# Attention and MLP on one core: the first 128 tokens of four batches ahead of everything, as the first MLP chunk

## The chip, the core, the metric

One NeuronCore of a Trainium2 chip runs the whole kernel. The metric is device time in microseconds (us), the median of several executions. A profile shows one execution; its span is 1.7 to 2.1 us shorter than that execution's time. Ratios are computed as the mean time of one kernel's runs over that of the other's runs of the same rounds, so they are not quite the ratio of the medians that I quote.

In the profile's lines PE is TensorE, PEld its weight loads, DVE VectorE, ACT ScalarE, POOL GpSimd, SP SyncE; a q behind the name is the queue that issues. The tiles: kq holds keys and queries in the layout of the scores, trqk their transposes before the copy, er the exps, pot the sum of PV, xn a centred tile, trx its transpose, xT the copy of that, ph and py the sums of the two MLP layers, hT the ReLU's output, yo the result. A name that ends in A belongs to the first 128 tokens. PSUM is the memory in which the kernel takes up TensorE's sums.

## The reference, cut to what matters

```python
# q, k, v: [8, 8, 576, 64]; s: [8, 8, 576]
scores = (q @ k.T) / sqrt(64)
cum = cumsum(max(s, 0))
bias = -(cum[..., :, None] - cum[..., None, :])          # 0 or less under the causal mask
attn = softmax(where(causal, -1e9, scores + min(bias, 0)))
x = (attn @ v) -> [8, 576, 512]                          # heads side by side
xn = (x - mean) / sqrt(var + 1e-6) * g_ln
out = x + relu(xn @ w_ch1) @ w_ch2                       # 512 -> 2048 -> 512
```

Token t needs keys 0 to t only, so the first 128 tokens of a batch need one block of 128 keys. An MLP needs all eight heads of a token, since it starts from a normalisation over 512 columns.

## The kernel before

Each engine has its own list of instructions in program order, fixed when the kernel is written; an engine that waits for one instruction does none of those behind it (the profile after shows TensorE idle for 1.86 us in such a place). The kernel walks through 64 heads (8 batches of 8). Per head TensorE does scores, later PV, and in between a few *units* of MLP work of an earlier batch, which are in a queue. A unit is four matmuls of 512 columns.

The first three batches bring q and k to the layout of the scores with transposes on TensorE ("pairs" of two heads) and copies out of PSUM. From batch 3 on this is done by DMA transposes.

```python
    for x, (kind, eng) in enumerate((("k", k_eng), ("q", q_eng))):   # qk_pair
        tr = (ps_m if g < 6 else ps_t).tile([P, S], BF16, name="trqk", ...)
        ... 6 transposes ...
        for w in range(2):
            copy_on(eng, dst[:, :, :, :, w], tr[w * D : (w + 1) * D, :]...)
...
def ln_xn(b):                       # all tiles of a batch at once, on VectorE
    for t, x in enumerate(x_tiles(b)):
        nc.vector.scalar_tensor_tensor(out=xn, in0=x, scalar=mvs[b][:, t, 0:1], in1=gb,
                                       op0=ALU.subtract, op1=ALU.mult)

def ln_tr(b, t):
    tr = ps_t.tile([P, KD, P], BF16, name="trx", tag="tr")    # pool of two PSUM buffers
    for kd in range(KD):
        nc.tensor.transpose(tr[:, kd, :], xn[:, kd * P : (kd + 1) * P], ident)
    nc.vector.tensor_copy(out=dst, in_=tr)
...
NU = {n: 3 for n in range(12, 20)}          # units per head: 4, but 3 in heads 12 to 19
for n in range(BH):
    ...
    if n < 10:                              # no MLP work yet: dummies keep TensorE busy
        scores(b, h); ...; keep_warm(2); ...; pv_next(); continue
    scores(b, h); run_units(1, True); ...; pv_next()
    for t in {2: (0, 1), 3: (2, 3, 4)}.get(h, ()) if b > 1 else ():
        ln_tr(b - 1, t); ...
    run_units(nu - 2)
    if b > 1 and h == 3:
        queue += batch_units(b - 1)         # 16 units of layer 1, 16 of layer 2
```

The last 64 tokens of the eight batches make a ninth chunk at the very end.

The softmax here doesn't subtract the row's maximum and nothing guards it: scores larger than these inputs give would overflow.

## Time and profile before

| | before |
|---|---|
| time, median of 3 | 389.0 us (388.33 to 389.14) |
| span of the profile | 385.7 us |
| first MLP matmul | 45.5 us |
| matmuls | 3016, of which 39 dummies |

From the page's part 4 (the chain that ended last, by engine) and part 5 (groups: line, engine, names, count, busy us, mean ns, idle time before and its releaser):

```profile
PE 80%; DMA 8%; DVE 5%; ACT 3%; SPq 1%; issue 1%; POOL 0%; ACTq 0%; DVEq 0%; POOLq 0%
...
L457 PE MATMUL py<-w_bf,hT 128*128 128x512 bf16 x576 | 137.9, 381 | 2.5 <-DVE yo L466 2.2
L439 PE MATMUL ph<-xT,w_bf 128*128 128x512 bf16 x512 | 123.2, 382 | 1.2 <-DVE hT L447 1.0
```

The chain runs through TensorE for four fifths of the span, and the two MLP layers have hardly any idle time in front of them. So what can be won is TensorE's lost time: before the MLP begins, and in the few waits after it.

Below, *useful stream* is the sum of all matmuls but dummies at the spacing that they show back to back (216 ns for 512 columns, and so on, as the prediction says), and *lost* is the time that is not useful stream. Where a trace misses matmul records (43 to 54 of some 3,050 in most of the later traces), I took the missing ones from the program's order and placed them behind the one before; so the sums are right, and an edge of a stage may be off by a few tenths of a us. (Counted again from the traces at the spacings said, the useful stream is some 2 us longer in both kernels, 337.3 in the one before, and the loss that much smaller in both; the differences between kernels stay within 0.4 us.)

### The profile page before, as it was taken

The numbers are of one execution on the slowest core, as the hardware profiler recorded it, in microseconds if no ns is written. First come the engines' busy times: TensorE is split into PE (matmuls) and PEld (weight loads), VectorE is DVE, ScalarE is ACT, GpSimd is POOL, SyncE is SP. The second block draws the span as 40 slices with busy tenths as digits, with TensorE's granted clock in tenths as the row PEclk, the third lists the DMA queues.
The fourth block names the chain that finished last, engine by engine and source line by source line (L and its number), as shares of the span: only waits on it lengthen the run. The fifth ranks groups of instructions, "written<-read, shape, count | busy, mean of one in ns | idle before, by whom it ended". The sixth has DMA issues, their size and how long they took to land.

```text
span 385.7 us, 8249 instructions
## 1 busy us (share of the span) xinstructions
PE 363.9 (94%) x3016; PEld 197.3 (51%) x3016; DVE 202.5 (53%) x538; ACT 194.5 (50%) x366; POOL 161.6 (42%) x442
## 2 busy tenths in 40 slices
PE   7878798997999999999999999999999979999994
PEld 2556455555555555565555555555555534444442
DVE  7557747768644754484356536743665473212211
ACT  7768667673874377427733773376346401411410
POOL 5861377437473365535565563456742110000000
PEclk9889899999999999999999999999999989999999
DMA  8799996178795599759887996589620011002013
GB/s 199 126 182 195 210 168 128 24 167 166 165 186 121 129 229 202 169 132 216 185 202 184 204 191 163 140 200 210 152 97 0 2 56 54 1 29 82 0 34 77
DMA packets 147777, 51.86 MB, mean 134 GB/s; under 512 B 134140, under 2 KB 142936, under 8 KB 147736
## 3 DMA queue, kind: packets, MB, share of 16 engines
q1 hardware_dynamic: 139352, 44.18, 50.5%
q0 software_dynamic: 8384, 7.15, 12.2%
q8 instruction: 24, 0.39, 0.4%
q14 instruction: 17, 0.14, 0.1%
HBM read 37.11 MB, written 9.44 MB: 121 GB/s over the span
## 4 chain that ended last, share of the span: by engine, by line
PE 80%; DMA 8%; DVE 5%; ACT 3%; SPq 1%; issue 1%; POOL 0%; ACTq 0%; DVEq 0%; POOLq 0%
PE py L457 31%; PE ph L439 30%; DMA vtmp<-in_v_dram 7%; PE pot L352 6%; PE sc L276 3%; PE sb L276 3%; PE sa L276 3%; PE trx L426 2%; ACT er L287 2%; DVE xn L410 2%; ACT kq L96 1%; DMA pairtmp<-in_q_dram 1%; PE trqk L229 1%; DMA kq<-c 1%; DVE yo L466 1%
## 5 line engine op out<-in xcount | busy, mean ns | idle before, releaser
L457 PE MATMUL py<-w_bf,hT 128*128 128x512 bf16 x576 | 137.9, 381 | 2.5 <-DVE yo L466 2.2
L439 PE MATMUL ph<-xT,w_bf 128*128 128x512 bf16 x512 | 123.2, 382 | 1.2 <-DVE hT L447 1.0
L449 ACT ACTIVATE hT<-ph 128x512 bf16<-128x512 f32 x107 | 63.9, 598 | 85.5 <-PE ph L439 85.5
L439 PEld LDWEIGHTS <-w_bf 128*128 128x128 bf16 x576 | 52.0, 98 | 55.2 <-issue 6.0
L457 PEld LDWEIGHTS <-hT 128*128 128x128 bf16 x576 | 52.2, 98 | 52.8 <-issue 4.0
L287 ACT ACTIVATE er<-sa 128x512 bf16<-128x512 f32 x64 | 38.1, 596 | 71.6 <-PE sa L276 44.8
L295 POOL TENSOR_SCALAR_AFFINE_SELECT er<-er 128x128 bf16<-128x128 bf16 x216 | 58.4, 294 | 33.3 <-ACT er L287 33.3
L447 DVE TENSOR_SCALAR hT<-ph 128x512 bf16<-128x512 f32 x37 | 25.6, 691 | 58.0 <-PE ph L439 54.9
L163 POOL CAST rows<-rowtmp 128x512 bf16<-128x512 f32 (+1 forms) x50 | 30.4, 607 | 44.3 <-DMA rowtmp<-in_q_dram 39.9
L352 PEld LDWEIGHTS <-er 128*128 128x128 bf16 x960 | 38.3, 99 | 17.9 <-DVE xm L369 3.1
L276 PEld LDWEIGHTS <-kq 68*128 68x128 bf16 x440 | 32.8, 98 | 27.6 <-DMA kq<-c 2.5
L360 DVE RECIPROCAL rinv<-pot 128x5 f32<-128x5 f32 x64 | 12.4, 194 | 61.5 <-PE pot L352 61.3
L352 PE MATMUL pot<-v_bf,er 128*128 128x65 bf16 x960 | 40.6, 195 | 2.3 <-DVE xm L369 1.8
L287 ACT ACTIVATE er<-sc 128x512 bf16<-128x512 f32 x64 | 39.1, 611 | 0.0
L100 POOL CAST v_bf<-vtmp 128x512 bf16<-128x512 f32 (+1 forms) x40 | 24.6, 620 | 32.9 <-DMA vtmp<-in_v_dram 32.5
L287 ACT ACTIVATE er<-sb 128x512 bf16<-128x512 f32 x64 | 38.3, 598 | 0.0
L466 DVE SCALAR_TENSOR_TENSOR yo<-py,rstd,xb 128x512 f32<-128x512 f32 x32 | 23.8, 748 | 25.5 <-PE py L457 20.3
L96 ACT COPY kq<-trqk 64x576 bf16<-64x576 bf16 x28 | 22.5, 802 | 11.9 <-PE trqk L229 11.7
L362 DVE TENSOR_TENSOR xb<-pot,rinv 128x256 f32<-128x256 f32 x64 | 27.2, 425 | 2.2
L276 PE MATMUL sa<-kq 68*128 68x512 bf16 x64 | 24.6, 385 | 3.0 <-DMA kq<-c 2.4
L276 PE MATMUL sc<-kq 68*128 68x256 bf16 (+1 forms) x208 | 25.2, 232 | 0.2
L386 DVE BATCH_NORM_STATS2 stats<-xb 128x6 f32<-128x128 f32 (+1 forms) x96 | 25.0, 320 | 0.4
(93 smaller groups left out, 302.2 us busy)
## 6 DMA issues: line engine op xcount, KB each, us to landing
vtmp<-in_v_dram SPq DMA_DIRECT2D x32, 256.0 KB
out_dram<-yo SPq DMA_DIRECT2D x32, 256.0 KB
rowtmp<-in_k_dram SPq DMA_DIRECT2D x40, 128.0 KB
rowtmp<-in_q_dram SPq DMA_DIRECT2D x40, 128.0 KB
w_bf<-in_moe_w_ch_dram POOLq DMA_DIRECT2D x8, 512.0 KB, 11.1
kp<-in_k_dram POOLq DMA_DIRECT2D x10, 144.0 KB, 4.4
qp<-in_q_dram POOLq DMA_DIRECT2D x10, 144.0 KB, 5.1
vtmp<-in_v_dram SPq DMA_DIRECT2D x8, 128.0 KB
```

Of the source, the lines that this page charges most:

```text
L96: nc.scalar.copy(out=out, in_=in_)
L163: nc.gpsimd.tensor_copy(out=r[0:pn, :, :, 0:D], in_=loaded.pop(("rows", gam, t))[0:pn])
L276: nc.tensor.matmul(a[:, c + a0 - q0 : c + a1 - q0], lhsT=k_cols(b, h, kb), rhs=cols, start=True, stop=not (pe_mask and diag),)
L287: nc.scalar.activation(out=e[:, o : o + 512], in_=a, func=ACT.Exp, scale=scale)
L295: nc.gpsimd.affine_select(out=e[:, o : o + P], in_=e[:, o : o + P], compare_op=ALU.is_ge, fill=0.0, base=0, pattern=[[1, P]], channel_mult ...
L352: nc.tensor.matmul(pot[:, t, :], lhsT=e[:, o : o + P], rhs=vv[:, kb, h, :], start=(kb == 0), stop=(kb == last),)
L362: nc.vector.tensor_tensor(out=xb[b][:, :, hs], in0=pot[:, 0:NF, 0:D], in1=rinv[:, 0:NF].unsqueeze(2).to_broadcast([P, NF, D]), op=ALU.mult,)
L439: nc.tensor.matmul(ph, lhsT=w1_bf[:, kd, fb * P : (fb + 1) * P], rhs=xT[:, kd, :], start=(kd == 0), stop=(kd == KD - 1),)
L447: nc.vector.tensor_scalar_max(out=hT[:, fb, :], in0=ph, scalar1=0.0)
L449: nc.scalar.activation(out=hT[:, fb, :], in_=ph, func=ACT.Relu)
L457: nc.tensor.matmul(py[0], lhsT=hT[:, fb, t * P : (t + 1) * P], rhs=w2_bf[:, fb, :], start=(fb == 0), stop=(fb == FB - 1),)
L466: nc.vector.scalar_tensor_tensor(out=yo, in0=py[0], scalar=rs, in1=x, op0=ALU.mult, op1=ALU.add)
```

## The change

The intent: have MLP work for TensorE as early as possible. The first 128 tokens of batches 0 to 3 are attended to first (32 small heads), which gives 512 finished rows, a full chunk. The rest of these batches then has 448 queries a head and chunks of three tiles. With that come: pairs for batch 3 too, VectorE's centring one tile at a time between units, more ReLU on VectorE in the first twelve heads, a pacing by what is left in the queue, and the last store issued by ScalarE. The core of the diff:

```diff
-    NPE = 3
-    NM = 10
+    NA = 4
+    NM = 12
@@ pairs: tokens 128 to 575 only; their transposes always in the pool of the transposed tiles @@
-            if g < 6:
-                tr = ps_m.tile([P, S], BF16, name="trqk", tag="m")
-            else:
-                tr = ps_t.tile([P, S], BF16, name="trqk", tag="tr")
+            tr = ps_t.tile([P, QT, QP], BF16, name="trqk", tag="tr")
@@ the start (cut) @@
+    bias_sum(0, P)
+    aug_first(0, nc.sync)
+    aug_first(1, nc.sync)
+    aug_first(2, nc.scalar)
+    first_qk(0, ("act", "dve", "act", "dve"))
+    ...
+    first_qk(1, ("dve", "act", "act", "act"))
+    keep_warm(4)
+    first_scores(0)
+    ...
+    first_qk(2, ("dve", "act", "act", "act"))
+    keep_warm(2)
+    first_scores(1)
+    first_x(0)
+    ...
+    first_tr(3)
+    queue += first_units()
@@ the loop (cut) @@
-            ln_xn(pb)
+            ln_xn(pb, 0)
...
+        end = next(m for m in (8 * i + 3 for i in range(1, B + 1)) if m >= n)
+        nu = -(-len(queue) // (end - n + 1))
...
+            elif h == 2:
+                ln_tr(b - 1, 0)
+                ln_xn(b - 1, 2)
+                run_units(1)
+                nu -= 1
+                ln_tr(b - 1, 1)
+                ln_xn(b - 1, 3)
...
-                nc.sync.dma_start(out=out[2 * t + 1, NF * P : S, :], in_=yo[TL:P])
+                nc.scalar.dma_start(out=out[2 * i + 1, NF * P : S, :], in_=yo[TL:P])
```

## The prediction

> **What bounds the kernel now.** I read the page first, then the windows by stage, the chain of waits, and the start of the timeline of TensorE. From the page, the totals and the slices:
>
> ```profile
> PE 363.9 (94%) x3016; PEld 197.3 (51%) x3016; DVE 202.5 (53%) x538; ACT 194.5 (50%) x366; POOL 161.6 (42%) x442
> ...
> PE   7878798997999999999999999999999979999994
> ...
> PEclk9889899999999999999999999999999989999999
> DMA  8799996178795599759887996589620011002013
> ```
>
> TensorE is the bound, but 94% flatters the start: there its busy time holds dummy matmuls (the idle tile) and the latency of single ones. So I counted work by the spacing of matmul starts in back-to-back runs: 216 ns for 512 columns, 56 for 128, 42 for 96, 28 for 64 or 65. All matmuls of the kernel before at this spacing make 343.7 us, of which 8.4 us are dummies: 335.3 us of useful stream in a span of 385.7, so 50.4 us is lost. The windows view cut at the stages (columns: stretch, its length, busy time and count of PE, PEld, DVE, ACT, POOL, granted clock, DMA share, GB/s):
>
> ```profile
> 0.00:45.50 45.50, 35.00 (x370) 21.33 (x371) 31.26 (x82) 33.61 (x57) 23.46 (x44) 0.92 1.03 179
> 45.50:60.00 14.50, 14.06 (x114) 7.54 (x113) 5.49 (x11) 10.12 (x20) 9.67 (x24) 0.88 1.12 193
> 60.00:100.00 40.00, 36.42 (x355) 21.03 (x352) 29.83 (x77) 24.28 (x44) 23.23 (x63) 1.00 0.58 121
> 100.00:310.00 210.00, 209.92 (x1866) 116.59 (x1865) 115.56 (x333) 112.11 (x223) 104.10 (x312) 1.00 0.70 157
> 310.00:325.00 15.00, 12.75 (x67) 6.34 (x66) 8.58 (x21) 0.00 (x0) 1.16 (x1) 0.89 0.14 54
> 325.00:385.70 60.70, 55.78 (x254) 24.42 (x252) 11.77 (x17) 14.33 (x24) 0.00 (x0) 0.98 0.13 40
> ```
>
> By the same count the loss is 27.6 us (8.4 of it dummies) before the first MLP matmul at 45.5 us, then 2.5, 6.3, 3.5 (of 210), 4.0 and 6.8 us; the last holds about 4.8 us of final add and store. The change can only win in the losses at the two ends. Two of them are named by the timeline of TensorE, an idle wait in brackets at the end of each:
>
> ```profile
> 24.46 0.38 PE L276 MATMUL sa<-kq 68*128 68x512 bf16 x1 [2.40 <-DMA kq<-c]
> 44.30 0.71 PE L426 MATMUL trx<-ident,xn 128*128 128x128 bf16 x8 [1.68 <-DVE xT L431]
> 90.88 0.41 PE L229 MATMUL trqk<-ident,kp 96*128 96x96 bf16 x6 [2.09 <-DVE xT L431]
> 314.81 1.18 PE L457 MATMUL py<-w_bf,hT 128*128 128x512 bf16 x4 [2.25 <-DVE yo L466]
> ```
>
> Until 45.5 us TensorE has only attention of batch 0 (a whole batch must be normalised before its MLP may start), each head waits for exp, copies or rows, and dummies fill up. At 90.88 and 314.81 VectorE does four or five normalisations in a row while TensorE waits.
>
> **What the skill says.** "TensorE: Matmul & The Clock Gate", Back-to-back issue gap, gives N/2.4 + 2.5 ns when warm; the trace agrees (216 ns for 512). The same page, What's actually happening, says that idleness halves the clock in windows of 3.4 us; the trace has three such windows before 50 us, at 0.5. "DMA: Bandwidth & Descriptors", Queues, rings and completion order, says that a DMA engine takes turns between queues, packet by packet. The trace agrees as far as one can count: between 30 and 45 us, with weights on GpSimd's queue and V on SyncE's, each moves about 165 packets a microsecond, so a V tile of 1024 small packets takes 6 us instead of its usual 1.5 to 2. The last point matters since the changed kernel asks for the weights earlier.
>
> **The change, part by part.**
>
> (1) Start. The first 128 tokens of batches 0 to 3 need only one key block (under the causal mask), so 32 heads of 128x128 make 512 finished rows, one full MLP chunk. What carries it is mostly ScalarE: per batch two exps of 512 columns (0.49 us spacing), three copies of 64x512 (about 0.72, from 0.80 for 64x576) and one 128x512 copy (0.5): 3.6 us. The bias rows can reach SBUF at about 13 us: in the kernel before they landed at 13.8 after a similar queue of loads. From there ScalarE has four pairs of exps (4.3 us), six copies of batches 2 and 3 (4.4), four transposed tiles (2) and the q copies of the first ordinary pair (1.3): 12 us, to 25. VectorE has 2.6 us per batch (two reciprocals 0.2, two 128x256 products 0.42, statistics 0.7, centring 0.67) after the second half of the prefix sum, and the last batch ends its path 3 to 4 us after its exp. I put the first MLP matmul at 28.5 us. Until then the useful stream is 7.3 us (32 scores, masks, 32 PV, transposes), so 21.2 us is lost against 27.6: gain 6.4.
>
> (2) Extra work of TensorE. Counted from the order of instructions: useful stream 337.7 us, 2.4 more. The mask is now added by matmul in 32 small heads plus 12 (+1.5), there are 32 transposes of 128 columns and 16 pairs instead of 12 (+1.9), the two helper sums with pick go (-1.0). Dummies fall from 39 to 23, which is inside the loss of (1). All MLP work is the same 36 tiles: 1st-layer matmuls of 384 columns for four chunks cost in proportion (161 ns).
>
> (3) Weights. The first chunk eats W1 in its first 16 units and the whole of W2 by unit 20. With three units a head and about 3.7 us a head (3x0.86 MLP, 0.6 scores, 0.4 PV, rest masks and transposes), unit 20 comes 6.5 heads after 28.5, at 52 us. GpSimd's queue must by then have moved 1024 packets of first tokens, 2240 of five pairs, 4096 of weights: 5120 large ones at 165 a us is 31 us, 2240 small ones at the 220 to 260 of mixed stretches about 9, together 40. It starts at 3 us and has a hole of some 6 us, since in GpSimd's order the casts of V and the power for rstd stand before the third quarter of W1. That gives 52 to 55 us. I book a stall of 3 us, and 0.5 us more loss than before in the rest of this first chunk (exp, ReLU and copies together fill ScalarE and VectorE).
>
> (4) Normalisation one tile at a time between MLP units, in 60 to 100 us and at 310. Of 6.3 us lost I give back 2.5 (the work of VectorE itself stays, and four batches with PE transposes load it and ScalarE to 80-90%); of 4.0 at the end 2.
>
> (5) The last store is issued by ScalarE beside SyncE: one issue of 0.59 us off the end, 0.5.
>
> (6) Batch 3 no longer goes through the ten DMA transposes and its row casts on GpSimd. Loss in that stretch is already small: 0.
>
> Sum: 6.4 - 2.4 - 3 - 0.5 + 2.5 + 2 + 0.5 = 5.5 us. The other stretches keep 3.5 and 6.3. That is about 380 us of span. Times run above spans (389.0 against 385.7), so 383.5. I set 381.5, 2 us lower: pacing by what is left in the queue, and vector help for ReLU in the first twelve heads, look made for just the stall that I booked.
>
> **The rivals.** (a) The weights become the bound. For: DMA share 1.03 and 1.12 to 60 us already, and V shares the engines. Against: the kernel before gets its last weights at under 60 us while it uses them at 70 to 79, so the traffic itself fits, and it left holes, one at 15 to 18 us. If unit 20 waits until 60 us, 8 us are lost instead of 3: 387. (b) ScalarE and VectorE become the bound in batches 0 to 3, since pair copies (0.80 for 64x576) now last to head 31. For: in 60 to 100 us VectorE is busy 29.8 of 40 us. Against: windows of 100 to 310 with 112 us of 210 on ScalarE lose next to nothing. It would cost 1 us per batch, 4 in all: 385. (c) All holes close: start 6.4, no stall, 45.5 to 60 gains 2, 60 to 100 gains 4.3, steady 1, end 2.5 and 0.5, less 2.4: 14 us, 375. (d) The head runs late, because rows for keys and queries queue behind four V tiles on SyncE's queue: every microsecond after 28.5 costs one; at 35 the gain is gone.
>
> **Range and chances.** Centre 381.5; (c) and (a) are close to the ends, so 374 to 388. The 2% line is 381.2, practically at the centre: faster 0.47, within 0.50, slower 0.03 (396.8 would need two of the rivals at full size).
>
> **What would show it.** First MLP matmul (ph) near 28.5 us, not after 33; the useful stream 337.7 by count; a wait of PE for DMA at the first py matmuls near 50 to 56 us of 0 to 6 us; in 60 to 310 almost no idle time of PE; no 2 us wait for yo near 310; the last store without a second issue on SyncE. I would be wrong if the chunk of batch 0 starts at 73 us or earlier, that is with no stall (then nearer 375), or if waits for er, kq or hT fill heads 0 to 31.

## The result, and the profile after

The changed kernel takes 398.0 us (median of 4, 397.52 to 398.98) against 388.66 in the same rounds (4 runs, 386.68 to 389.14). The ratio is 1.0253, with a 95% interval of 1.0211 to 1.0296: slower by 2.5%. Executions over 1.5% slower than the fastest of the same kernel are left out of the means. The span is 395.8 us, 10.1 more. From its page, the totals, slices and the chain:

```profile
PE 364.9 (92%) x3011; PEld 206.6 (52%) x3054; DVE 212.8 (54%) x561; ACT 202.7 (51%) x400; POOL 161.3 (41%) x412
...
PE   5677999979999998999989999999999989999995
...
PEclk8585999989999999999999999999999999999998
DMA  8993996263236259889999999799830001002012
...
PE 67%; DVE 9%; DMA 9%; ACT 5%; SPq 4%; issue 3%; POOL 3%; POOLq 0%; ACTq 0%
```

TensorE carries only 67% of the chain, where it was 80%. Its clock stood at half for much of the first four slices (5 and 8 in the row of PEclk); before, these were 9 and 8. The windows of the changed kernel, in the columns of the prediction's windows:

```profile
0.00:37.00 37.00, 23.58 (x155) 13.75 (x158) 23.76 (x56) 17.72 (x29) 18.47 (x38) 0.70 0.97 152
37.00:80.00 43.00, 42.63 (x389) 25.12 (x394) 24.84 (x64) 28.10 (x55) 16.20 (x25) 0.98 0.82 136
80.00:120.00 40.00, 35.56 (x334) 22.47 (x336) 28.27 (x73) 25.74 (x53) 19.34 (x45) 0.96 0.41 74
120.00:190.00 70.00, 67.46 (x660) 42.09 (x665) 43.69 (x122) 46.23 (x99) 37.77 (x100) 1.00 0.73 144
190.00:280.00 90.00, 86.38 (x798) 49.75 (x808) 48.40 (x142) 50.46 (x103) 55.48 (x166) 1.00 1.00 198
```

From 37 to 80 us the idea works: TensorE is busy 42.6 of 43 us. But then it isn't full again until 280 us, where the kernel before was full from 100 us on (209.9 of 210). In us lost per stage, dummies counted as loss:

| | 0-37 | 37-80 | 80-120 | 120-200 | 200-280 | 280-end | sum | useful stream |
|---|---|---|---|---|---|---|---|---|
| before | 22.4 | 10.5 | 4.0 | 1.2 | 1.3 | 11.0 | 50.4 | 335.3 |
| changed | 29.0 | 1.8 | 8.9 | 4.3 | 5.6 | 8.5 | 58.1 | 337.7 |

By 80 us the changed kernel has lost 30.8 us against 32.9, a gain of 2.1 that the 2.4 us of extra work eat. The end gains 2.5. By the clock, the 10 us are made between 80 and 280 us: 18.7 lost against 6.5. The same stretch of time holds other heads in the two kernels, though: heads 12 to 19 run from 60 to 99 us before and from 89 to 125 us now. The part on why the prediction was wrong counts by heads.

**The start.** The chain of the changed kernel up to its first MLP matmul (start us, us, what):

```profile
11.59 4.08 DMA kA<-c
...
23.04 0.75 DVE xn L453
...
24.07 0.59 DVE kA L107
24.69 0.72 ACT kA L105
25.43 0.72 ACT qA L105
26.17 0.72 ACT qA L105
26.91 0.61 ACT er L604
...
37.40 1.51 PE ph L489 x4
```

The bias rows land at 15.7 us. From there it is a relay: VectorE normalises batch 0 (it ends at 23.8), only then comes the key copy of batch 3, which stands behind it in VectorE's order, then three copies on ScalarE one after another, then the exps of batch 2, then the normalisation of batch 2. The two engines take turns where I had summed each alone.

**The boundaries.** VectorE around 80 us, where the batch's next chunk is prepared, and what TensorE waited for then (both timelines; in brackets the idle time before, and its releaser):

```profile
80.19 0.43 DVE L107 COPY xT<-trx 128x512 bf16<-128x512 bf16 x1
80.65 1.19 DVE L453 SCALAR_TENSOR_TENSOR xn<-xb,mv,gb 128x512 bf16<-128x512 f32 x1
81.76 0.74 DVE L516 SCALAR_TENSOR_TENSOR yo<-py,rstd,xb 128x512 f32<-128x512 f32 x1
82.42 0.41 DVE L107 COPY xT<-trx 128x512 bf16<-128x512 bf16 x1
82.75 1.31 DVE L107 COPY kq<-trqk 64x448 bf16<-64x448 bf16 x2
```

```profile
82.88 0.49 PE L252 MATMUL trqk<-ident,qp 112*128 112x112 bf16 x4 [1.86 <-DVE xT L107]
```

The second copy of a transposed tile (xT) could be made at 80.6, but a centring and an output stand before it in VectorE's order. TensorE needs its PSUM buffer for the next transposes and waits until 82.8. Directly after, the clock is granted at half for 3.4 us. The same wait comes at the next two boundaries (0.64 and 0.85 us at 118 and 152 us, with 0.23 and 0.35 for the keys just before).

**The end.** The last two stores of the changed kernel are issued at once by two queues, as wanted:

```profile
391.95 0.47 SPq L547 DMA_DIRECT2D out_dram<-yo  x1
391.95 0.50 ACTq L548 DMA_DIRECT2D out_dram<-yo  x1
```

### The profile page after: what moved, and what is told of

Read it like the earlier page. It is cut to its first block, busy times and chain, and to the rows that moved or that the text cites. A ratio compares the mean times of both kernels' runs of the same rounds, so it can differ in the third digit from the quotient of the medians.

```text
span 395.8 us, 8269 instructions
## 1 busy us (share of the span) xinstructions
PE 364.9 (92%) x3011; PEld 206.6 (52%) x3054; DVE 212.8 (54%) x561; ACT 202.7 (51%) x400; POOL 161.3 (41%) x412
## 4 chain that ended last, share of the span: by engine, by line
PE 67%; DVE 9%; DMA 9%; ACT 5%; SPq 4%; issue 3%; POOL 3%; POOLq 0%; ACTq 0%
PE py L507 25%; PE ph L489 23%; PE sab L322 8%; PE pot L395 5%; SPq L165 3%; DMA rowtmp<-in_q_dram 3%; DVE xn L453 2%; DMA vtmp<-in_v_dram 2%; ACT er L335 2%; PE trqk L252 2%; ACT kq L105 2%; DMA kp<-in_k_dram 1%; DVE yo L516 1%; DMA kq<-qA 1%; PE trx L461 1%
## 5 line engine op out<-in xcount | busy, mean ns | idle before, releaser
L489 PE MATMUL ph<-xT,w_bf 128*128 128x512 bf16 (+1 forms) x562 | 123.9, 356 | 3.7 <-ACT hT L499 1.4
L335 ACT ACTIVATE er<-sab 128x512 bf16<-128x512 f32 (+1 forms) x192 | 97.3, 583 | 52.7 <-PE sab L322 50.1
L499 ACT ACTIVATE hT<-ph 128x512 bf16<-128x512 f32 (+1 forms) x113 | 62.1, 554 | 77.4 <-PE ph L489 77.2
L507 PEld LDWEIGHTS <-hT 128*128 128x128 bf16 x576 | 51.6, 98 | 48.7 <-issue 0.3
L497 DVE TENSOR_SCALAR hT<-ph 128x512 bf16<-128x512 f32 (+1 forms) x47 | 30.3, 645 | 54.5 <-PE ph L489 52.4
L322 PE MATMUL sab<-kq 68*128 68x448 bf16 (+4 forms) x352 | 47.9, 263 | 0.6 <-DMA kq<-qA 0.3
L403 DVE RECIPROCAL rinv<-pot 128x4 f32<-128x4 f32 (+1 forms) x64 | 12.1, 188 | 59.0 <-PE pot L395 58.7
L516 DVE SCALAR_TENSOR_TENSOR yo<-py,rstd,xb 128x512 f32<-128x512 f32 x32 | 23.9, 748 | 31.8 <-PE py L507 20.1
L322 PEld LDWEIGHTS <-kq 68*128 68x128 bf16 x352 | 27.8, 99 | 21.0 <-DMA kq<-qA 1.4
L177 POOL CAST qA<-rowtmp 128x512 bf16<-128x512 f32 (+1 forms) x40 | 24.3, 608 | 32.8 <-DMA rowtmp<-in_q_dram 29.2
L105 ACT COPY kq<-trqk 64x448 bf16<-64x448 bf16 x38 | 25.0, 659 | 24.4 <-PE trqk L252 22.9
L405 DVE TENSOR_TENSOR xb<-pot,rinv 128x192 f32<-128x192 f32 (+1 forms) x64 | 25.0, 391 | 2.2
L453 DVE SCALAR_TENSOR_TENSOR xn<-xb,mv,gb 128x512 bf16<-128x512 f32 x28 | 21.4, 767 | 0.1
L461 PE MATMUL trx<-ident,xn 128*128 128x128 bf16 x144 | 14.8, 229 | 4.5 <-DVE xn L453 3.0
```

The lines of the kernel that those rows point to most:

```text
L105: nc.scalar.copy(out=out, in_=in_)
L322: nc.tensor.matmul(a[:, c + a0 - q0 : c + a1 - q0], lhsT=k_cols(b, h, kb), rhs=cols, start=True, stop=not (pe_mask and on_diag),)
L335: nc.scalar.activation(out=e[:, o : o + width], in_=a[:, 0:width], func=ACT.Exp, scale=scale)
L405: nc.vector.tensor_tensor(out=xb[b][:, t0:NF, hs], in0=pot[:, t0:NF, 0:D], in1=rinv[:, t0:NF].unsqueeze(2).to_broadcast([P, NF - t0, D]), ...
L453: nc.vector.scalar_tensor_tensor(out=xn, in0=x, scalar=mean, in1=gb, op0=ALU.subtract, op1=ALU.mult)
L489: nc.tensor.matmul(ph[:, 0:n], lhsT=w1_bf[:, kd, fb * P : (fb + 1) * P], rhs=xT[:, kd, 0:n], start=(kd == 0), stop=(kd == KD - 1),)
```

## The experiments

Sixteen kernels ran besides the changed one, every one correct. The times are medians of 4, each with the kernel before in the same rounds. The loss by stage, from one profile of each, is counted as above:

| | time | before | 0-37 | 37-80 | 80-120 | 120-200 | 200-280 | 280-end | first MLP matmul |
|---|---|---|---|---|---|---|---|---|---|
| changed | 398.0 | 388.7 | 29.0 | 1.8 | 8.9 | 4.3 | 5.6 | 8.5 | 37.2 |
| xn_all | 397.1 | 387.9 | 28.7 | 3.2 | 7.8 | 3.6 | 4.4 | 9.4 | 37.0 |
| trqk_m | 414.4 | 387.9 | 28.5 | 8.7 | 8.6 | 15.8 | 4.1 | 8.8 | 36.2 |
| rows_first | 395.5 | 387.9 | 27.8 | 2.4 | 7.4 | 5.4 | 4.3 | 8.3 | 34.7 |
| copies_split | 398.9 | 387.9 | 28.5 | 2.5 | 9.6 | 4.6 | 5.1 | 8.7 | 36.3 |
| xt_act | 391.6 | 389.4 | 27.1 | 2.2 | 5.5 | 4.9 | 2.8 | 8.1 | 33.7 |
| k_act | 397.1 | 389.4 | 29.1 | 2.7 | 9.5 | 4.6 | 4.9 | 8.7 | 37.5 |
| head_all | 396.0 | 389.4 | 27.1 | 3.1 | 8.6 | 4.7 | 4.5 | 8.7 | 33.6 |
| head_xt_xn | 390.9 | 389.4 | 25.5 | 3.5 | 5.4 | 5.5 | 1.8 | 8.9 | 31.8 |
| warm | 398.0 | 388.8 | 25.5 | 4.6 | 7.9 | 5.0 | 7.2 | 8.6 | 33.6 |
| warm_head_xt | 388.8 | 388.8 | 24.7 | 3.8 | 4.8 | 5.0 | 3.1 | 8.1 | 32.5 |
| batch3_dma | 393.6 | 388.6 | 28.3 | 1.9 | 5.9 | 6.9 | 1.8 | 8.4 | 35.9 |
| before_xt | 385.3 | 388.8 | 23.5 | 11.2 | 2.3 | 1.8 | 0.9 | 9.4 | 48.3 |
| before_plus | 382.3 | 388.8 | 22.0 | 11.4 | 2.1 | 1.2 | 1.3 | 6.7 | 46.1 |
| before_tiles | 387.5 | 388.6 | 22.6 | 11.5 | 3.8 | 1.4 | 1.1 | 6.8 | 47.9 |
| before_nu3 | 394.3 | 388.6 | 22.4 | 9.9 | 4.0 | 5.6 | 5.2 | 9.7 | 45.7 |
| before_nu4 | 391.2 | 388.6 | 22.6 | 8.6 | 9.7 | 1.1 | 1.2 | 11.3 | 45.8 |

### Boundaries: when to centre (xn_all)

```diff
-            ln_xn(pb, 0)
+            for i in range(5):
+                ln_xn(pb, i)
             ln_rstd(pb)
```

and the later calls of ln_xn go.

> The changed kernel with one part undone: all tiles of a batch are centred at once after its last head, as in the kernel before, instead of one by one between MLP units. Theory B1 (centring tile by tile puts the transposed-tile copies late in VectorE's order, so TensorE's transposes of the next pair wait for a PSUM buffer at every batch boundary): the 12 us lost between 80 and 280 us shrink by 4 to 7, while the end near 310 to 330 loses 1 to 2 us again; 392 to 395 against 398. Rival (the boundary waits come from the shared PSUM buffers whenever the centring is done): no change within 1 us there, 398 to 400.

Measured: 397.1 us (393.94 to 397.74). Between 80 and 280 us the loss is 15.8 instead of 18.7, at the end 0.9 more. The forecast of 392 to 395 was missed. Centring tile by tile has a part in it, 3 us at most by this one profile and 1 by the times; the boundary waits stay (2.9 us for copies of transposed tiles), so it isn't the main cause.

### Boundaries: which PSUM pool (trqk_m)

```diff
-            tr = ps_t.tile([P, QT, QP], BF16, name="trqk", tag="tr")
+            tr = ps_m.tile([P, QT, QP], BF16, name="trqk", tag="m")
```

> The changed kernel with the transposes of the ordinary q/k pairs written to the PSUM pool of the MLP (two buffers) in place of the pool of the transposed tiles. Theory B2 (the waits of pair transposes for the copy of a transposed tile, 2.0+1.2+1.5 us, and the half-clock window of 3.4 us after the first, are the cost of sharing that pool): 4 to 6 us less, 392 to 394. Rival (VectorE's own order is late, and TensorE will wait for the same copies one matmul later; or ph and py now wait for the pool): within 2 us of 398.

Measured: 414.4 us, 16 slower. My theory fell, and the rival held in its first half and more. The timeline of TensorE says why:

```profile
128.14 0.36 PE L252 MATMUL trqk<-ident,qp 112*128 112x112 bf16 x4 [3.49 <-DVE kq L107]
```

It no longer waits for the copy of a transposed tile, but for the key copy, which stands even later in VectorE's order. One of the two MLP buffers is held by an open sum, so the query transposes need the buffer of the key transposes at once. So in either pool TensorE waits for a copy that VectorE makes late. That the buffers were not scarce as well is not shown: no run gave the pool a third one.

### Boundaries: who copies the transposed tiles (xt_act)

```diff
-        transposed(xns.pop((b, t)), dst, "dve")
+        transposed(xns.pop((b, t)), dst, "act")
```

> The changed kernel with the copies of transposed tiles (128x512, some 0.42 us on VectorE) on ScalarE. Theory B3 (at each batch boundary VectorE's fixed order holds normalisation, output and key copies ahead of these copies, and TensorE waits; ScalarE sits idle 5 us at the first boundary): the loss between 80 and 280 us, 18.7 us in the changed kernel, falls by 4 to 6 us; 392 to 394 against 398. Rival (the copies on ScalarE push back the exps, and TensorE waits for those): within 1.5 us of 398.

Measured: 391.6 us (390.45 to 392.22), 6.4 less than the changed kernel: theory B3 holds. What the pair transposes waited for in the whole run (us in total, times, longest), first in the changed kernel, then in this one:

```profile
PE trqk L252 <- DVE xT L107: 3.9, 5, 1.9
```

```profile
PE trqk L252 <- ACT xT L105: 2.1, 4, 0.7
```

Of the second, 0.7 us are in the start, which is not edited: ScalarE makes these copies there in the changed kernel too. The windows over 80 to 280 us, first of the changed kernel, then of this one:

```profile
80.00:120.00 40.00, 35.56 (x334) 22.47 (x336) 28.27 (x73) 25.74 (x53) 19.34 (x45) 0.96 0.41 74
...
200.00:280.00 80.00, 76.38 (x686) 43.01 (x697) 43.57 (x127) 42.81 (x86) 49.53 (x147) 1.00 0.99 198
```

```profile
80.00:120.00 40.00, 37.57 (x375) 23.37 (x374) 26.08 (x70) 30.77 (x65) 20.27 (x49) 1.00 0.45 80
...
200.00:280.00 80.00, 79.01 (x723) 44.13 (x722) 39.60 (x114) 47.59 (x95) 50.77 (x148) 1.00 0.98 194
```

TensorE gains 2.0 and 2.6 us of busy time, VectorE loses 2 to 4, ScalarE takes 5 more, and TensorE still waits 1.4 us for its copies from 75 us on; the half clock after 80 us is gone. By count the loss between 80 and 280 us falls from 18.7 to 13.3. In this one profile the start was also some 3 us quicker, although nothing in it was edited. That looks like luck of the run, and the four times may hold some of it: by heads, and with the start left out, the profile gains 3.5 us, so the copies' own part lies between 3.5 and the 6.4 of the times. The clock was granted at half for 6.8 of the first 39 us here, against 24, but that amount alone doesn't set the start: xn_all and k_act, with the same start, had 11.4 and 12.2 us of it and began the MLP at 37.0 and 37.5.

### Boundaries: the key copy on ScalarE (k_act)

```diff
-            qk_pair(g, "act" if h == 1 and b else "dve", "act")
+            qk_pair(g, "act" if h in (1, 3) and b else "dve", "act")
```

> The changed kernel with the key copies of the pair at head 3 of a batch (1.31 us) on ScalarE in place of VectorE. If it is VectorE's total load near a boundary that counts, some 2 to 3 us less in 80 to 155 us, 395 to 396. If it is the place of the transposed-tile copies in VectorE's order, which come before this copy, next to nothing: 397 to 398.5.

Measured: 397.1 us (395.99 to 398.93). Three pairs of copies, 1.3 us each, were taken off VectorE, and it gave 0.9 us, which is no more than the spread. That speaks for the place of an instruction in VectorE's order and against its total load, but they are only three copies, and xt_act took load off VectorE too: the two are not fully told apart.

### Start: the bias rows first (rows_first)

```diff
-    for b in range(1, NA):
-        ld_v(b, 0)
     nc.vector.memset(c_one, 1.0)
 ...
     aug_first(2, nc.scalar)
+    for b in range(1, NA):
+        ld_v(b, 0)
```

> The changed kernel with the bias rows of the first tokens sent before the V tiles of batches 1 to 3 on SyncE's queue. Theory A (the start is one serial chain, and its first link is the landing of these rows at 15.7 us): the first scores start near 11 to 12 us, the first MLP matmul comes 3 to 4 us earlier than 37.4, and the whole is 394 to 395. Rival A' (after 40 us the weights decide: the first chunk waits for W2, which lands near 60 us): the first MLP matmul comes earlier but the second layer starts no earlier than 58 us, and the whole stays within 1 us of 398.

Measured: 395.5 us (392.77 to 397.71). The first scores come at 12.1 us instead of 15.8, 3.7 earlier, the first MLP matmul 2.5 earlier; the second layer starts at 56.9 us instead of 58.5. The time is 2.5 less, though the spread of 5 us makes this a weak number. The missing 1.2 us went to a wait of 4.4 us of TensorE for the keys of batch 3, whose load GpSimd issues only after a cast of V, and V now lands later.

### Start: no two engines on one tile (copies_split)

```diff
-    first_qk(0, ("act", "dve", "act", "dve"))
+    first_qk(0, ("act", "act", "dve", "dve"))
...                                             # the same for batches 1 to 3
```

> The changed kernel with the two copies of the keys of the first tokens both on ScalarE and those of the queries both on VectorE, so that no two copies to interleaved columns of one tile are on different engines. Theory A2 (a copy on ScalarE waits for the copy on VectorE that writes the same tile, 5.3 us in three waits, and the copies of one batch run one after another): 1 to 2 us per batch of the last three goes, the first MLP matmul comes 2 to 4 us earlier, 394 to 396. Rival: VectorE, which now has one copy more per batch, becomes the longer arm: within 1 us of 398.

Measured: 398.9 us (397.25 to 400.33); the first MLP matmul at 36.3. The rival held: ScalarE's waits for VectorE's copies were in the profile, 5.3 us of them, but with two copies per batch VectorE becomes the longer arm. A wait that is seen is not a wait that ends the chain.

### Start: a better order (head_all)

rows_first, and besides:

```diff
     ld_first(2)
+    ld_first(3)
     cast_v(0, 0, "pool")
     cast_v(1, 0, "pool")
-    ld_first(3)
 ...
     first_qk(1, ...)
+    first_qk(2, ...)
     keep_warm(4)
     first_scores(0)
 ...
-    first_qk(2, ...)
+    first_qk(3, ...)
     keep_warm(2)
     first_scores(1)
```

> The changed kernel with the start reordered: bias rows before the V tiles of batches 1 to 3, loads of the first tokens of batch 3 before the casts of V, transposes and copies for batches 2 and 3 one step earlier. Theory A (the start is a chain of waits in a fixed order, not of too much work): first MLP matmul near 29 to 31 us against 37.2 and 34.7 with the rows alone, and the whole 6 to 8 us less than the changed kernel, 390 to 392. Rival A' (the weights take over): the second layer still starts at 56 us or later, the whole is 394 to 396.

Measured: 396.0 us (395.82 to 396.23), 2 less than the changed kernel. The first MLP matmul came at 33.6, not 29 to 31. The transposes of batch 2 now stand before the first scores and wait for their loads and buffers, so the scores start at 15.2 us although the rows are there. Two thirds of my theory's gain are missing.

### Start and boundaries together (head_xt_xn)

head_all, xt_act and xn_all in one.

> The reordered start, the copies of transposed tiles on ScalarE, and all tiles of a batch centred at once. If the two theories add up (start 6 to 8, boundaries 5 to 7), 384 to 387, at or just below the kernel before (387 to 389); if both gains are eaten by the weights or by ScalarE, 391 or more.

Measured: 390.9 us (390.26 to 392.68). Given xt_act's 391.6, the start and the centring added next to nothing to the time, though the MLP starts 5 us earlier than in the changed kernel. The gains don't add up.

### Start: the clock (warm)

53 dummies more (the expectation says 47, a miscount: 76 against 23), at the places where TensorE waits in the start, for instance:

```diff
-    keep_warm(4)
+    keep_warm(14)
     first_scores(0)
```

> The changed kernel with 47 more dummy matmuls in the start, in places where TensorE waits anyway. Theory C (the half clock, granted for 24 of the first 39 us in the profiled run, stretches the chain of small matmuls and transposes of the start): granted clock near 1.0 up to 37 us, first MLP matmul at 33 to 35 us instead of 37.2, the whole 394 to 396. Rival (the chain is made of copies, exps and normalisation, which have no such clock; dummies only stand in the way): the first MLP matmul at 37 us or later, 398 to 400.

Measured: 398.0 us (396.29 to 398.83), and yet the theory is right on the start. The window of the start, the next, and then what TensorE waited for:

```profile
0.00:33.50 33.50, 28.99 (x207) 15.33 (x211) 23.70 (x56) 17.46 (x29) 17.40 (x37) 1.00 0.99 167
33.50:80.00 46.50, 42.90 (x398) 25.46 (x404) 27.72 (x69) 28.11 (x56) 19.37 (x30) 1.00 0.81 131
```

```profile
PE py L507 <- DMA w_bf<-in_moe_w_ch_dram: 1.2, 1, 1.2
```

The clock is full up to 37 us, and the MLP starts at 33.6 instead of 37.2. The rival is right in one thing: ScalarE's copies in the start take the same 0.72 to 0.73 us under half and under full clock. But now the second layer waits 1.2 us for W2, which it never did in the changed kernel. At the first boundary (79.9 us for the transposes that came at 82.9) the kernel is still 3 us ahead. In this profile they are given back by a half clock of 6.8 us after that boundary instead of 3.4, another of 3.4 us at 204, and a wait of 2.2 us for a DMA transpose. Whether that is chance or a rule I can't tell from one profile; the four times say that nothing was left of the 3 us.

### All that helped (warm_head_xt)

head_all, xt_act and 36 more dummies (not 39, as the expectation says).

> The changed kernel with the reordered start, 39 more dummies in it, and the copies of transposed tiles on ScalarE. If start, clock and boundary add up: first MLP matmul at 29 to 31 us and 385 to 388. If the order of the start is bound by VectorE's four normalisations whatever the clock, first MLP matmul at 32 us or later and 390 to 392.

Measured: 388.8 us (388.45 to 389.18), ratio 1.0003: level with the kernel before, 9 us better than the changed kernel. The start is at 32.5 us, with half clock for only 3.4 us of it; the order of the start is what is left as a limit, and TensorE waits 1.5 us for W2.

### The same cure for the kernel before (before_xt, before_plus)

```diff
-        nc.vector.tensor_copy(out=dst, in_=tr)
+        nc.scalar.copy(out=dst, in_=tr)
```

> The kernel before with the copies of transposed tiles on ScalarE, nothing else. It has one wait of TensorE for such a copy of 2.1 us at 90.9 us and smaller ones near 42 to 44 us. If theory B3 holds for it too, 2 to 4 us less: 385 to 387. If ScalarE's exps are pushed back in the steady stretch, where the loss is only 3.5 us in 210, the same or up to 3 us more.

Measured: 385.3 us (384.31 to 386.04), ratio 0.991 (0.9871 to 0.995). The loss between 80 and 120 us falls from 4.0 to 2.3, and 280 to the end from 11.0 to 9.4. In the start the same move costs: TensorE waits 2.9 us for a copy on ScalarE, where it waited 1.7 for VectorE, and the first MLP matmul comes at 48.3 us instead of 45.5. Leaving the first batch's copies on VectorE was not tried.

before_plus adds two parts of the change: the last batch alone is centred tile by tile between MLP units, and the second of two last stores goes through ScalarE.

> The kernel before with three small parts: copies of transposed tiles on ScalarE, the last batch alone centred tile by tile between MLP units, and the second of each two last stores issued by ScalarE. Expected from the parts: 2 to 4 for the copies, 2 for the hole of 2.4 us near 312, 0.5 for the store: 382 to 385, faster than both kernels. If the holes only move, 387 to 389.

Measured: 382.3 us (381.64 to 382.68), ratio 0.9838 (0.9797 to 0.988): faster than both kernels, by 1.6% than the one before, which is clear of noise but under the 2% at which a run counts as faster. The end now loses 6.7 us instead of 11.0, and the timeline of TensorE between 302 and 318 us has not one wait. The two parts of the change alone are worth 3.0 us (385.3 to 382.3).

### Centring in all batches (before_tiles)

before_plus with the changed kernel's order of ln_xn from batch 1 on:

```diff
-            ln_xn(pb, 0, 1 if pb == B - 1 else 9)
+            ln_xn(pb, 0, 1 if pb else 9)
```

> The faster variant of the kernel before (382.3) with the tile-by-tile centring in all batches from batch 1 on, not the last alone. If this part by itself costs at the boundaries, 1 to 3 us more, 383.5 to 385.5; if it is harmless where heads are long, 382 to 383.

Measured: 387.5 us (384.02 to 391.90, of which the slowest was a slow run); the profiled one, the fastest of them, is 2.4 us longer in span than before_plus (382.3 against 379.9). The loss between 80 and 120 us is 1.7 higher, and elsewhere the same. Its three fast runs took 384.02, 386.75 and 388.19 us, against 381.64 to 382.68 of before_plus: 4.5 us more by the medians, rather more than the 1 to 3 expected, and the runs are less even. The spread doesn't allow more.

### Length of a head (before_nu3, before_nu4)

```diff
-    NU = {n: 3 for n in range(12, 20)}
+    NU = {n: 3 for n in [*range(12, 20), *range(28, 52)]}     # before_nu3
+    NU = {}                                                   # before_nu4
```

> The kernel before with three MLP units instead of four in heads 28 to 51 (the work moves to a longer tail), so heads of some 3.8 us without pair transposes. If short heads as such leave the other engines no room at the boundaries, 3 to 6 us of new loss in the three batches, 392 to 395. If not, the time stays at 388 to 390 and the changed kernel's boundary loss belongs to the pairs.

Measured: 394.3 us (393.45 to 396.81), 5.7 more, with nothing else changed. (Head 3 of each batch keeps four units, so it is 25 units in eight heads instead of 32; a head takes 4.3 us, and took 4.7.) The windows of the kernel before, and then of this one:

```profile
120.00:200.00 80.00, 80.00 (x716) 44.49 (x714) 43.88 (x128) 41.37 (x83) 41.48 (x126) 1.00 0.81 181
200.00:280.00 80.00, 80.00 (x723) 44.81 (x721) 46.11 (x134) 41.52 (x84) 44.49 (x128) 1.00 0.80 179
```

```profile
120.00:200.00 80.00, 76.74 (x727) 43.71 (x738) 50.73 (x146) 43.00 (x87) 47.11 (x132) 1.00 0.89 189
200.00:280.00 80.00, 76.58 (x688) 42.89 (x700) 44.53 (x127) 40.51 (x82) 46.72 (x136) 1.00 0.79 170
```

A stretch that was full for 160 us loses 3.3 and 3.4 us of TensorE's busy time, without a single pair transpose and with all tiles centred at once. Its waits are of all kinds; from 120 to 280 us the longest are 2.7 us for DMA transposes, 0.7 each for ReLU on ScalarE and for VectorE's scaling of the PV sum, 0.6 for a mask on GpSimd and 0.5 for ReLU on VectorE. By count the loss from 120 to 280 us is 10.8 against 2.5. The changed kernel has 9.9 there, with other waits: 2.7 us in all for copies of transposed tiles, 0.3 for a DMA transpose or its rows. Shorter heads are enough to make a loss of that size; that they make it in the changed kernel too is not shown.

> The kernel before with four units in heads 12 to 19 too, where it has three. If its loss of 6.3 us between 60 and 100 us comes from short heads with pairs, 2 to 3 us less, 386 to 387; if the hole at 90.9 us stays, the same.

Measured: 391.2 us (387.83 to 392.58), no gain. The loss from 60 to 80 us falls from 2.8 to 1.3, but from 80 to 120 us it rises from 4.0 to 9.7, of which some is a half clock granted from 91 to 101 us. Whether longer heads would pay there stays open.

### Batch 3 by DMA again (batch3_dma)

xt_act with the bound for pairs, their loads and rows back at three batches:

```diff
-        if h % 2 == 1 and g < 4 * NA:
+        if h % 2 == 1 and g < 4 * NPE:        # NPE = 3, in all seven places
```

> The changed kernel with the copies of transposed tiles on ScalarE (391.6 by itself) and with batch 3 prepared by DMA transposes again, as in the kernel before. If pair transposes and copies of batch 3 cost what is left, 2 to 4 us less, 388 to 390; if they cost nothing (step 6 of the prediction), 391 to 392; if DMA transposes with the loads of that stretch cost more, 393 or more.

Measured: 393.6 us (391.34 to 394.22) against 391.6 for xt_act. The pairs of batch 3 are not what is left; they even help a little. (By heads, 28 to 35 lose 5.4 us here and 0.9 in xt_act, while 20 to 27 and 36 to 51 lose 3.6 us less.)

Two parts of the change were not tested alone: ReLU on VectorE in the first twelve heads, and the pacing by the queue.

## Why the prediction was wrong

I predicted 381.5 us and a gain of 2% as likely as not; it is a loss of 2.5%. I counted the loss once more, cut at the same heads in every kernel; a head is taken to begin with VectorE's reciprocal for the PV that stands in it. In us, from the recount named above:

| | to the first MLP matmul | from there to head 12 | heads 12-19 | 20-27 | 28-35 | 36-43 | 44-51 | 52-59 | rest | sum |
|---|---|---|---|---|---|---|---|---|---|---|
| before | 27.3 | 2.6 | 6.0 | 0.7 | 0.4 | 0.4 | 0.4 | 0.4 | 10.3 | 48.3 |
| changed | 28.5 | 5.6 | 4.3 | 3.1 | 0.9 | 3.2 | 1.9 | 0.4 | 7.8 | 55.7 |
| xt_act | 25.4 | 5.0 | 3.7 | 2.2 | 0.9 | 2.0 | 1.7 | 0.4 | 7.4 | 48.7 |
| before_nu3 | 26.4 | 1.8 | 6.0 | 0.7 | 2.6 | 2.2 | 4.4 | 0.5 | 9.1 | 53.7 |

Against the kernel before, the prediction had 6.4 us less in the first column, 3.5 more in the second, 2.5 less in heads 12 to 19 (its 60 to 100 us), nothing in heads 20 to 59, and 2.5 less in the rest. Measured are 1.2 more, 3.0 more, 1.7 less, 7.2 more and 2.5 less. So two terms carry the miss: the start, by 7.6 us, and heads 20 to 51, by 7.2. By its own steps:

**Step 1, the start, failed.** It put the first MLP matmul at 28.5 us from the sum of ScalarE's work after the rows landed at 13. It came at 37.2, and 28.5 us were lost until then, not 21.2. The rows landed at 15.7 (2.7 us). From there the MLP was 15.5 us away by the prediction and 21.5 in the trace; under full clock it was 19.0 (warm, rows at 14.6). So of the other 6.0 us some 3.5 are the relay between ScalarE and VectorE (the sum of one engine is a lower bound for a chain that changes engines at each step), and some 2.5 the half clock, as far as one profile of each tells. I had used spacings at full clock for a stretch that I had myself emptied of work. The rival (d) of the prediction named the direction, but its rule, that each us of the start costs one of the whole, is wrong: starts earlier by 2.5, 3.6 and 3.6 us (rows_first, warm, head_all) were worth 2.5, 0 and 2.0.

**Step 2, the extra work, was right,** but it is no forecast: 337.7 us is a count of the program.

**Step 3, the weights, was right in kind,** and its total by luck. Its own sum, 3 + 40 + 6, gives 49 us and not the 52 to 55 it names, so the stall rested on a slip. W2's last quarter landed at 62.2 us, and the 3 us of stall did not come, as the late start gave W2 time; the 3.0 us more up to head 12 are mainly the first boundary, with its wait of 1.86 us and the half clock after it. When the MLP began at 31.8 to 33.7 us, the stall was there in three kernels of five, with 1.2 to 1.6 us (warm, warm_head_xt, head_xt_xn).

**Step 4, the centring, was near in heads 12 to 19** (1.7 us less of 2.5) **and failed at every other boundary.** In the sum, "the other stretches keep 3.5 and 6.3". Instead heads 20 to 51 lost 9.1 us, where they had lost 1.9, and the first boundary, which the kernel before passes with no MLP work under way, came on top. There are two causes to name, and the first is shown: the copies of transposed tiles stood behind centring and outputs in VectorE's order. On ScalarE they cost 3.5 us less by heads, start left out, and 6.4 by the times (xt_act).

The second, that heads got shorter, is not shown. Eight heads share 28 units instead of 32, and layer-1 units have 384 columns. Such a shortening costs the kernel before 8.0 us in heads 28 to 51 (before_nu3: 9.2 against 1.2). But the likeness is one of sums. Heads 28 to 35 of the changed kernel, its shortest with 3.9 us each, lose only 0.9 us; heads 44 to 51, which have their 32 full units again, lose 1.9. With xt_act heads 20 to 51 still lose 6.8 us against 1.9, and what makes these 4.9 us stays open; I could not lengthen the heads of the changed kernel without giving it more MLP work than it has. The rival (b) saw ScalarE and VectorE as the bound and priced it at 4 us. What I held against it, that 100 to 310 us lose next to nothing, was read off heads of four full units, and did not carry over to the heads that the change makes.

At the end step 4 was right: 300 to 330 us lose 2.0 us instead of 4.4 (2 predicted). **Step 5** is right in kind, but smaller: from the end of the last yo to the end of the span it is 3.9 us instead of 4.1, 0.2 and not 0.5. The two together gave 3.0 us on the kernel before against 2.5 in the sum. **Step 6**, nothing for batch 3, is right within 2 us.

The account closes: 7.7 us more lost and 2.4 more work are the 10.1 us of span. The centre of 381.5 was 2 us below what the steps themselves summed to (383.5), for a help in pacing and ReLU that no line backed.

## What to carry to other kernels

Filler work that one stretch is given is taken from another: before moving it, look at how much room per step the other engines need in the stretch that gives it up, and test that by shortening the steps of the old kernel, which is a one-line edit. In a fixed order it counts where an instruction stands, and not only how busy its engine is; move the small copy that frees a buffer to the engine that is idle at that moment. The sum of one engine's work is no estimate for a start in which two engines hand each other every tile. And compare two kernels by pieces of work, not by stretches of time: by the clock the loss seemed to begin at 80 us, by heads half of the miss was in the start.

## What the Trainium skill lacked or had wrong

- "TensorE: Matmul & The Clock Gate", Back-to-back issue gap: it gives some 81 ns (128 columns) and 131 ns (512) as the sustained spacing of pairs of weight load and matmul. Here each matmul has its own weight load, and the sustained spacing is 56 and 216 ns in every trace, which is the page's formula for the isolated gap.
- The same page, HAM oscillation — how this bites in real kernels: the rule of no idle gaps over some 3.4 us, taken alone, is too mild. The changed kernel had the half clock for 24 of its first 39 us, and the longest wait in its timeline there was 2.7 us; and it got it for 3.4 us right after a single wait of 1.9 us that ended at 82.9 us, while one of 2.1 us at 90.9 us brought the kernel before none. 53 more dummies (warm) kept the clock full through the start.
- No page: how much a shorter step between full stretches costs the other engines. Here 24 heads with 25 MLP units in eight heads instead of 32 (before_nu3) made the kernel 5.7 us slower.
